# Moving the first quarter of W_in ahead of the keys of pair 1 in POOL's load order

## The chip, the cores and the metric

The kernel runs on one core of one Trainium2 chip. The metric is the device time of one execution in microseconds (us), as the median of several runs. A profiled execution also has a span: the time from its first to its last instruction on the core.

## What is computed

A gated recurrence over 768 steps in 4 batches and 8 heads of 48 channels makes y; y is the input x of a two-layer network with a gelu (tanh form) between the layers.

```python
for t in range(S):                       # S = 768
    state = alpha[:, :, t, :, None] * state + einsum('bhd,bhe->bhde', k[:, :, t], v[:, :, t])
    y[:, :, t] = einsum('bhd,bhde->bhe', q[:, :, t], state)
x = y.transpose(0, 2, 1, 3).reshape(B * S, H * D)      # 3072 x 384
h = x @ w_in                                           # w_in: 384 x 2048
g = 0.5 * h * (1 + tanh(c * (h + 0.044715 * h**3)))
out = g @ w_out                                        # w_out: 2048 x 384
```

All inputs and the output are float32. The kernel computes in bf16 and f16 with float32 sums.

## The kernel before

**Tiling.** The 768 steps are cut into 6 chunks of 128, and the 4 batches into two pairs of batches. A "pair" in the names of this kernel is one chunk of two batches, so there are 12: pair 0 and pair 1 are the first chunk of batches 0, 1 and 2, 3. For each pair the recurrence is done in chunked form:

- ACT takes the logarithm of alpha (`ln`), PE sums it along the chunk (`cum`), and ACT makes the exponentials `b`, `binv` and `bend`.
- DVE multiplies q by `b` and k by `binv` (`qp`, `kp`, line 354). For pairs 0 and 1 this is one instruction for each half of a pair, so two `qp` and two `kp`.
- PE transposes `qp` and `kp` (`qkT_ps`, line 364), and DVE or ACT copies the result from PSUM to SBUF (`qkT`, line 382).
- PE multiplies them (`at`, line 424), DVE masks (`atm`, line 431), PE makes y (`yps`, lines 470 and 473), ACT or DVE copies it to `x` (480), PE transposes it (`xT_ps`, 487) and DVE copies that to `xT` (491).
- For the state, the k of pairs 0 and 1 is turned back (`k_ps` on PE, 390; `kn`, 397) and multiplied with v (`kv`, 441).

**The network.** Layer 1 of a pair is 16 groups of three matmuls into `hT` (line 497), each followed by a gelu on ACT (`gT`, 503). Group `nt` uses columns of W_in from part `nt // 4`: W_in is loaded in four parts ("in 0" to "in 3"), and W_out likewise ("out 0" to "out 3"). Layer 2 (`acc`, 516) sums over the 16 groups.

**Who sets the order.** A planner, `Scheduler.order()`, runs when the program is built. Each task has a cost for the engines it can run on, a priority, and tasks and buffers that it waits for. Walking through estimated times, the planner fixes the order of all instructions on each engine. PE also gets filler matmuls (`idle`, line 222) where the plan has a gap early on. On the chip each engine then follows its own fixed list and waits on semaphores.

**Loads.** The pieces in `RINGS` are issued by the SP and ACT queues, in the order of that list: alpha, q and k of pair 0, then alpha and q of pair 1. All other loads are issued by POOL in the order of the tuple `LOADS`. Its names are read so:

- `gatea0` and `gatek0` are small copies on POOL that read a loaded tile (line 255), so that POOL issues nothing further before alpha, respectively k, of pair 0 has landed.
- `v0` is v of pair 0 (line 235). `pk1` is k of pair 1, in four pieces (`load_packed`, line 247). `in 0` is the first part of W_in (`load_w`, line 262).
- Numbers are the further pairs; `2a` and `2b` are halves of pair 2.

The planner numbers the loads in this order and gives each a time at which it lands:

```python
    if t.land is not None:
        wire = max(wire, t.end + W["dma"] - t.land) + t.land
        t.done = wire + t.late
```

**Buffers.** `BUFS` holds two PSUM buffers of tag `yk`: transposes of q and k, of x, the y and the kv all share these two, so a transposition waits until the last but one has been copied out. The tag `ff` (layer 1, layer 2, the filler) has four.

Of the kernel before, what the change touches and what calls it, by code (L numbers as in the profile page):

```python
# [136 lines left out]
class _Kernel:  # L137
# [3 lines left out]

    SPLIT = (2,)
    EARLY = (0, 1)
    LOADS = ('gatea0', 'v0', 'gatek0', 'pk1', 'in 0', 'in 1', 'in 2', 'v1', 'in 3', 'out 0', 'out 1', '2a', 'out 2', '2b', 'out 3', '3', '4', '5', '6', '7', '8', '9', '10', '11')

    PACKED, CUM_FF, R = (0, 1), (1,), 4
    RINGS = (('a', 0, 0, 'SP'), ('a', 0, 2, 'ACT'), ('a', 0, 1, 'SP'), ('a', 0, 3, 'ACT'), ('q', 0, 0, 'SP'), ('q', 0, 2, 'ACT'), ('q', 0, 1, 'SP'), ('q', 0, 3, 'ACT'), ('k', 0, 0, 'SP'), ('k', 0, 2, 'SP'), ('k', 0, 1, 'SP'), ('k', 0, 3, 'SP'), ('a', 1, 0, 'SP'), ('a', 1, 1, 'SP'), ('a', 1, 2, 'SP'), ('a', 1, 3, 'SP'), ('q', 1, 0, 'SP'), ('q', 1, 1, 'SP'), ('q', 1, 2, 'SP'), ('q', 1, 3, 'SP'))
# [389 lines left out]
    def tasks(self):  # L537
# [28 lines left out]
        for r, m, j, e in self.RINGS:  # L566
            loads[r, m, j] = s.add("load", {e: W["piece_issue"]}, n, self.load_packed(r, *pairs[m], j), land=W["piece"] + (0 if n else W["begin"]))
            n += 1
            if (r, m, j) == self.TABLE:
                s.add("table", {"ACT": W["table"]}, n, lambda e: self.act_set(LN_EXP))  # L570
        for step in self.LOADS:
            if step[0] == "v":
# [257 lines left out]
```

## Time and profile before

| what | value |
|---|---|
| median of 6 runs | 185.33 us (184.52 to 186.07) |
| the profiled execution, its time | 185.15 us |
| the profiled execution, its span | 183.4 us |
| PE (TensorE matmuls) busy | 175.7 us, 96% of the span |
| ACT (ScalarE) busy | 136.1 us, 74% |
| DVE (VectorE) busy | 104.8 us, 57% |
| POOL (GpSimd) busy, mostly issuing loads | 61.1 us, 33% |
| chain that ended last | PE 86%, DMA 8% |
| TensorE clock granted | 1.0 throughout |

"Busy" is time in instructions; PE overlaps instructions, so its share is not the share of its peak. The chain follows the execution back from its last instruction, at each step to what released it. The profile can also be asked for stretches of time, which is needed here: everything that the change touches lies in the first 30 us.

### The profile page before, as it was taken

What the parts mean: (1) busy time and instruction counts of PE and PEld (TensorE: products, weight loads), DVE (VectorE), ACT (ScalarE), POOL (GpSimd) and SP (SyncE); (2) the same over time, 40 slices, a digit from 0 to 9 for tenths busy, and PEclk for the clock granted to TensorE, in tenths of its full rate; (3) what the DMA queues carried; (4) which work ended last, traced back from release to release, by engine and by line L of the source; (5) the groups of instructions that cost most, each with busy time, mean ns of one, the idle gap of its engine ahead of it and who ended that gap; (6) DMA issues with size and microseconds to landing.
All of it is one profiled execution on the core that took longest, in us unless ns stands there. A gap on an engine that the chain in (4) does not pass through costs nothing.

```text
span 183.4 us, 4630 instructions
## 1 busy us (share of the span) xinstructions
PE 175.7 (96%) x1862; PEld 129.1 (70%) x1862; DVE 104.8 (57%) x232; ACT 136.1 (74%) x310; POOL 61.1 (33%) x68
## 2 busy tenths in 40 slices
PE   7886999999999999999999999999999999999993
PEld 2464868666686787688688769678677677686873
DVE  7776864065869896597499798298644715000000
ACT  3665979855888789859799768899789884491941
POOL 2599445985655556556660200000000000000000
DMA  5999999999999999999999985753271290311102
GB/s 141 202 235 176 187 227 205 205 220 170 188 275 187 165 226 195 179 226 202 180 211 231 186 205 119 104 114 68 51 168 49 43 202 4 88 43 46 43 0 86
DMA packets 51205, 27.76 MB, mean 151 GB/s; under 512 B 38832, under 2 KB 48240, under 8 KB 51184
## 3 DMA queue, kind: packets, MB, share of 16 engines
q0 software_dynamic: 32096, 17.70, 69.9%
q1 hardware_dynamic: 18512, 9.38, 21.6%
q10 hardware_dynamic: 576, 0.39, 0.7%
q8 instruction: 14, 0.23, 0.6%
q14 instruction: 7, 0.06, 0.1%
HBM read 25.17 MB, written 4.72 MB: 163 GB/s over the span
## 4 chain that ended last, share of the span: by engine, by line
PE 86%; DMA 8%; ACT 1%; POOL 1%; SPq 1%; DVE 0%; issue 0%; DVEq 0%; POOLq 0%
PE acc L516 34%; PE hT L497 33%; DMA k<-in_k_dram 5%; PE at L424 4%; PE qkT_ps L364 4%; PE yps L473 2%; PE yps L470 2%; PE kv L441 2%; PE cum L320 2%; DMA qkT<-kp 2%; DMA a<-in_alpha_dram 1%; PE xT_ps L487 1%; POOL k L247 1%; ACT L503 1%; PE cum L322 1%; SPq L247 1%
## 5 line engine op out<-in xcount | busy, mean ns | idle before, releaser
L497 PE MATMUL hT<-xT,w_in 128*128 128x256 bf16 x576 | 70.6, 273 | 0.4 <-ACT gT L503 0.4
L503 ACT ACTIVATE gT<-hT 128x256 bf16<-128x256 f32 x192 | 63.7, 386 | 8.8 <-PE hT L497 8.2
L516 PE MATMUL acc<-w_out,gT 128*128 128x384 bf16 (+1 forms) x400 | 68.8, 319 | 0.0
L497 PEld LDWEIGHTS <-w_in 128*128 128x128 bf16 x576 | 53.9, 98 | 8.2 <-issue 0.6
L516 PEld LDWEIGHTS <-gT 128*128 128x128 bf16 x400 | 36.8, 98 | 19.6
L431 DVE TENSOR_TENSOR atm<-at,ut 128x512 bf16<-128x512 f32 x48 | 31.0, 686 | 15.6 <-PE at L424 15.1
L354 DVE TENSOR_TENSOR qp<-q,b 128x768 bf16<-128x768 f32 (+1 forms) x15 | 11.8, 795 | 17.7 <-ACT b L343 13.8
L528 ACT COPY ot<-acc 128x384 f32<-128x384 f32 (+1 forms) x18 | 8.3, 462 | 13.9 <-PE acc L516 12.7
L235 POOL DMA_DIRECT2D v<-in_v_dram x13 | 14.6, 1123 | 9.6 <-PE hT L497 2.7
L235 POOL DMA_DIRECT2D k<-in_k_dram x11 | 12.2, 1108 | 11.3 <-DVE kp L354 4.6
L343 ACT ACTIVATE b<-cum 128x768 bf16<-128x768 f32 (+1 forms) x15 | 10.2, 684 | 6.6 <-PE cum L322 2.6
L235 POOL DMA_DIRECT2D q<-in_q_dram x11 | 12.2, 1112 | 7.3 <-DMA k<-in_k_dram 2.0
L235 POOL DMA_DIRECT2D a<-in_alpha_dram x11 | 12.2, 1112 | 6.4 <-DMA k<-in_k_dram 1.9
L213 ACT ACT_TABLE_LOAD x9 | 11.5, 1283 | 2.8 <-issue 2.6
L354 DVE TENSOR_TENSOR kp<-k,binv 128x768 bf16<-128x768 f32 (+1 forms) x15 | 11.7, 793 | 1.2 <-DMA k<-in_k_dram 0.9
L458 DVE TENSOR_TENSOR st<-stmp,bend 64x192 bf16<-64x192 f32 x32 | 11.3, 353 | 1.5
L456 DVE TENSOR_TENSOR stmp<-kv,st 64x192 f32<-64x192 f32 x32 | 11.3, 352 | 1.0 <-PE kv L441 0.7
L503 ACT ACT_TABLE_LOAD x9 | 11.5, 1283 | 0.2
L480 ACT CAST x<-yps 128x384 bf16<-128x384 f32 x15 | 7.2, 481 | 5.2 <-PE yps L473 5.1
L222 PE MATMUL idle<-zero 128*128 128x512 bf16 x28 | 9.6, 449 | 1.2 <-DVE blk L778 1.2
L382 DVE COPY qkT<-qkT_ps 128x1024 bf16<-128x1024 bf16 (+1 forms) x14 | 9.2, 687 | 2.4 <-PE qkT_ps L364 2.4
L343 ACT ACTIVATE binv<-cum 128x768 bf16<-128x768 f32 (+1 forms) x15 | 10.1, 683 | 0.0
(62 smaller groups left out, 160.2 us busy)
## 6 DMA issues: line engine op xcount, KB each, us to landing
out_dram<-ot SPq DMA_DIRECT2D x23, 192.0 KB, 3.5
a<-in_alpha_dram POOLq DMA_DIRECT2D x9, 384.0 KB, 13.1
q<-in_q_dram POOLq DMA_DIRECT2D x9, 384.0 KB, 13.4
k<-in_k_dram POOLq DMA_DIRECT2D x9, 384.0 KB, 13.3
v<-in_v_dram POOLq DMA_DIRECT2D x11, 192.0 KB, 13.4
w_in<-in_moe_w_in_dram POOLq DMA_DIRECT2D x4, 384.0 KB, 8.6
w_out<-in_moe_w_out_dram POOLq DMA_DIRECT2D x4, 384.0 KB, 11.3
a<-in_alpha_dram SPq DMA_DIRECT2D x6, 96.0 KB, 3.3
```

The lines of the kernel that those rows point to most:

```text
L213: nc.scalar.add_instruction(mybir.InstLoadActFuncSet(name=nc.get_next_instruction_name(), act_func_set_id=i, engine=mybir.EngineType.Activ ...
L222: self.nc.tensor.matmul(ps, self.zero[:, 0:self.C], self.zero, start=True, stop=True)
L235: (nc.sync if e == "SP" else nc.gpsimd).dma_start(u[n][:, lo:hi].rearrange("t b h d -> t (b h) d"), src)
L343: self.nc.scalar.activation(u[n].rearrange("t i h d -> t i (h d)")[:, lo:hi], cum, AF.Exp, scale=1.0 if n == "b" else -1.0)
L354: self.nc.vector.tensor_tensor(out, rows, b, op=ALU.mult)
L382: self.copy(e)(t, ps)
L431: self.nc.vector.tensor_tensor(u["atm", i][:, o], u["at", i][o], self.ut[:, None, :].to_broadcast([self.C, self.H // 2, self.C]), op=ALU.mult)
L456: nc.vector.tensor_tensor(s[ps], acc, old[ps, :, fs], op=ALU.add)
L458: nc.vector.tensor_tensor(new[ps, :, fs], acc, u["bend"][ps, i, :, None].to_broadcast([64, H // 2, D]), op=ALU.mult)
L497: self.nc.tensor.matmul(h, self.w_in[:, j, nt * self.C:(nt + 1) * self.C], self.xT[c][:, j, lo:hi].rearrange("p g t -> p (g t)"), start=j ...
L503: return lambda e: self.nc.scalar.activation(self.gT[c % self.NG][:, nt, lo * self.C:hi * self.C], f.pop(("h", c, lo, nt)), AF.Gelu_apprx_ ...
L516: self.nc.tensor.matmul(f["acc", c, b][:, lo:hi], self.gT[c % self.NG][:, nt, b * self.C:(b + 1) * self.C], self.w_out[:, nt, lo:hi], star ...
```

## The change

One name moves in the tuple `LOADS`: `'in 0'` goes ahead of `'pk1'`, so POOL issues the first part of W_in directly behind `gatek0`, ahead of the four pieces of k of pair 1.

```diff
     SPLIT = (2,)
     EARLY = (0, 1)
-    LOADS = ('gatea0', 'v0', 'gatek0', 'pk1', 'in 0', 'in 1', 'in 2', 'v1', 'in 3', 'out 0', 'out 1', '2a', ...
+    LOADS = ('gatea0', 'v0', 'gatek0', 'in 0', 'pk1', 'in 1', 'in 2', 'v1', 'in 3', 'out 0', 'out 1', '2a', ...
```

The description that came with the change says that the order of all engines stays. The built programs differ in more than POOL's loads, because the planner now has another landing time for k. Those are all the differences:

| engine | before | after |
|---|---|---|
| POOL | k of pair 1 x4, W_in 0, 1, 2 | W_in 0, k of pair 1 x4, W_in 1, 2 |
| DVE | qp, kp, xT, kp, xT, qp (qp and kp of pair 1, xT of pair 0) | qp, qp, xT, kp, xT, kp |
| PE | transposes of qp, 2 fillers, transposes of kp, layer 1, transposes of qp, layer 1, transposes of kp | transposes of qp, 2 fillers, transposes of qp, layer 1, transposes of kp, layer 1, transposes of kp |

"Layer 1" stands for one group of three matmuls each time. ACT and SP keep their lists.

More of the change, by code (lines that the diff above doesn't have):

```diff
@@ L143 @@
     EARLY = (0, 1)
-    LOADS = ('gatea0', 'v0', 'gatek0', 'pk1', 'in 0', 'in 1', 'in 2', 'v1', 'in 3', 'out 0', 'out 1', '2a', 'out 2', '2b', 'out 3', '3', '4', '5', '6', '7', '8', '9', '10', '11')
+    LOADS = ('gatea0', 'v0', 'gatek0', 'in 0', 'pk1', 'in 1', 'in 2', 'v1', 'in 3', 'out 0', 'out 1', '2a', 'out 2', '2b', 'out 3', '3', '4', '5', '6', '7', '8', '9', '10', '11')
     PACKED, CUM_FF, R = (0, 1), (1,), 4
```

## The prediction

> **What bounds the kernel now.** The page comes first: TensorE (PE) is busy for 175.7 of 183.4 us, and the chain that ended last is 86% PE and 8% DMA. The DMA share is where loads can still set the end, so I follow the chain in order of time from the start. Its columns are start in us, length in us, what.
>
> ```profile
> 8.56 1.62 POOL k L247 x3
> 10.19 5.77 DMA k<-in_k_dram
> 15.95 0.03 issue
> ...
> 16.08 0.56 DVE kp L354
> 16.64 0.28 DVE xT L491
> 16.91 0.04 issue
> 16.95 0.38 PE qkT_ps L364 x4
> 17.34 0.43 PE idle L222 x2
> ...
> 19.84 0.33 PE hT L497 x3
> 20.16 0.33 PE at L424 x8
> ...
> 24.66 0.01 issue
> 24.68 0.50 PE hT L497 x3
> ```
>
> The last of the four pieces of k of pair 1, issued by POOL, lands at 10.19 + 5.77 = 15.96. From 16.95 on the chain stays on PE, without a gap over 0.04 us up to 28.7, where layer 1 of pair 1 runs. So a shift of PE at 20.16 (the first `at` of pair 1) has no idle time to sink into. It also meets no later load: the DMA pieces left in the whole chain are the first alpha, these two of k (5%) and the transposes qkT<-kp near the end, which move with PE.
>
> The timeline of VectorE (DVE) shows what k holds up (start, length, what, the wait ahead of it in brackets):
>
> ```profile
> 14.57 0.56 DVE L354 TENSOR_TENSOR qp<-q,b 128x384 bf16<-128x384 f32 x1 [0.97 <-ACT x L480]
> 16.08 0.56 DVE L354 TENSOR_TENSOR kp<-k,binv 128x384 bf16<-128x384 f32 x1 [0.94 <-DMA k<-in_k_dram]
> 16.55 0.35 DVE L491 COPY xT<-xT_ps 128x384 bf16<-128x384 bf16 x1
> 16.82 0.55 DVE L354 TENSOR_TENSOR kp<-k,binv 128x384 bf16<-128x384 f32 x1
> 17.28 0.35 DVE L491 COPY xT<-xT_ps 128x384 bf16<-128x384 bf16 x1
> 17.55 0.55 DVE L354 TENSOR_TENSOR qp<-q,b 128x384 bf16<-128x384 f32 x1
> 18.11 1.89 DVE L382 COPY qkT<-qkT_ps 128x512 bf16<-128x512 bf16 x3
> ```
>
> Both xT copies stand behind a kp, though their inputs were transposed by 15.7. They gate the first layer-1 product of pair 0 at 18.07. Hence **k of pair 1 gates layer 1 of both pairs**.
>
> The timeline of POOL gives the issues:
>
> ```profile
> 8.54 2.20 POOL L247 DMA_DIRECT2D k<-in_k_dram  x4
> 10.73 2.25 POOL L262 DMA_DIRECT2D w_in<-in_moe_w_in_dram  x3
> ```
>
> With the times to landing of the DMA view, the first part of W_in lands at 10.73 + 6.5 = 17.2, the second at 19.5, the third at 21.4 (starts 11.47 and 12.23; POOL waits for them at 19.81 and 21.68). So part 0 lands 0.9 us before its first use. Earlier arrival buys nothing unless xT comes earlier too.
>
> **What the skill says.** "DMA: Bandwidth & Descriptors", section "Queues, rings and completion order": each DMA engine takes its queues in turn, and within a queue descriptors are consumed in ring order. The trace agrees in the order of landings on POOL's queue: k, then W_in 0, 1, 2. Its section "Anatomy of one DMA — SWDGE (gpsimd) path" prices a POOL load at 2.0 us plus bytes / 436e3; an estimate for 96 KB of k is 2.2 us. The trace shows 5.1 to 6.0, so these loads stand in a line and the fit is only a floor. "PSUM — Partial Sum Buffer", section "Engine vs sequencer instructions", calls the vector engine's queue strictly first in, first out; the xT at 16.55 behind the waiting kp agrees.
>
> **The change part by part.**
>
> 1. POOL: one issue of W_in (756 ns) goes ahead of four issues of k (551 to 572 ns). W_in 0 is issued at 8.54, k at 9.29 to 11.5 instead of 8.54 to 10.73. Sum unchanged, so W_in 1 starts as before at 11.47. Nothing on SP's queue or ACT's is moved, but the four q pieces that SP issues from 7.42 to 9.27 (landed by about 14.4, 5.1 to 5.6 us each) now share the DMA engines with W_in 0 rather than k. POOL reuses a completion semaphore every eighth load, so W_in 3 (14.17) will wait for W_in 0 instead of the first k piece (13.7). W_in 0 should land near 15, so W_in 3 is issued some 0.8 us later. Its data stand behind W_in 1, 2 and v until 22.8, which covers that; without the cover the product at 24.68 would be 0.8 late.
>
> 2. When does k land now, called K? It is behind 384 KB of W_in. Low bound: only the issue counts, 15.96 + 0.75 = 16.7. Even lower, if the line is shorter once q has drained: last issue 10.94 plus the shortest time of a piece, 5.1, gives 16.0. If bytes are conserved, the pair of loads ends when it ended before, K = 17.2. High bound: a full spacing of two W_in loads (17.2 to 19.5 is 2.3) is put ahead of k, K = 18.3. W_in 0 had landed only 1.3 behind k where its successors need 1.9 to 2.3, so part of it had already moved while k finished; that head start is lost to k. I take **K = 17.5**, between 17.2 and 15.96 + 1.9 = 17.9.
>
> 3. The planned order does move, on DVE and PE, against the plain reading of "stays": the second qp and one xT go ahead of both kp (qp, qp, xT, kp, xT, kp), and both groups of qp transposes ahead of those of kp. From K on, with the pitches of the DVE timeline: kp at K + 0.13, second xT K + 0.60 to 0.95, kp K + 0.87 to 1.42. PE: qp transposes at K + 0.99 (the buffer is freed by that xT), product K + 1.29, kp transposes K + 1.62, product K + 1.84, last kp transposes K + 2.17. DVE copies: 0.60 apart from K + 1.42, the last ends at K + 3.3. PE after 2.17: 0.29, product 0.33, k_ps 0.27, product 0.33, then `at` at **K + 3.4**. Before it was 20.16 = K + 4.2. So 0.8 us goes from behind k to ahead of it: the first qp transposes (0.39) and the fill (0.43) are done during the wait. They were paid before too.
>
> 4. Sum: `at` moves by 17.5 + 3.4 − 20.16 = **+0.74 us**, and the end with it. ACT's table load, 17.98 before, can start near 16.9 and stays hidden; the first gelus wait for PE. The profiled execution took 185.15 with a span of 183.4, 0.18 below the median of 185.33. I expect a span of 184.1, a time of 185.9 for such an execution and a median of **186.1**.
>
> The formula has one unknown: shift = K − 16.76. The 0.5% that a measurement of this kernel can tell from no change is 0.93 us: slower needs K over 17.7, faster K under 15.8.
>
> **The rivals.**
>
> A, the forecast: a shared line, K between 17.2 and 17.9, 185.8 to 186.5. For it: landings in order and 1.9 to 2.3 apart. Chance 0.50, of which 0.13 lies above 17.7.
>
> B, a full load ahead: q slows W_in 0 and k then pays a whole spacing, K near 18.3, shift +1.54, 186.9. It ends on the slow side, and decides from K = 17.7. For it: q's pieces and W_in 0 overlap from 10 to 14, a window that moved 221 to 246 GB/s, and k no longer gets its share there. Against: the same bytes were done by 17.2. Chance 0.28.
>
> C, latency rather than bytes: K = 16.7, shift −0.06, 185.3; the issue's 0.75 is just paid by the work moved ahead. Against: times to landing growing from 5.1 to 10.5 along the line. Chance 0.14.
>
> D, the wait shrinks: with q out of the way k's pieces land quickly and K falls below 15.8, shift −1 or more, 184.3. Around 5 us SP's k pieces took 3.1 us to land; but then W_in 0 would have to be through by 13, within a microsecond of v's landing (5.0 + 7.2 = 12.2). Chance 0.08, of which 0.03 remains within 0.5%.
>
> That the early part changes nothing it was loaded for is in all four: its first product stays behind k, through xT.
>
> **How the numbers follow.** Slower: 0.13 of A and 0.28 of B, plus 0.03 for noise along the rest of PE's chain, 0.44. Faster: 0.05 of D and 0.02 of noise, 0.07. Within: 0.49. The range goes from C less 0.2 of spread (the six runs lie within 0.8 of the median) to B, rounded: 185.1 to 187.0.
>
> **What would show it.** In the profile after: k's landing in the chain near 17.5 (15.96 before); DVE with two qp and an xT ahead of the waiting kp; its wait for k about 1.6 us from 15.9 (0.94 before); the first layer-1 product near K + 1.3, 18.8 instead of 18.07; `at` near 20.9; the pair-1 products and everything after later by that. A landing near 16.7 makes C right, over 17.7 B. It would be wrong in kind if `at` moved and the end did not (slack I didn't see after 28.7), or if the end moved with `at` at its place.

## The result and the profile after

| | before | after |
|---|---|---|
| median of all runs | 184.97 us (70 runs) | 185.81 us (33 runs) |
| ratio after / before, 95% interval | | 1.0032 [1.0017, 1.0047] |
| profiled execution, its time | 185.15 us | 186.63 us |
| profiled execution, its span | 183.4 us | 184.9 us |

The change makes the kernel 0.3% slower. That is clear of noise, and below the 0.5% within which the forecast placed it. The profiled execution is one of the longer ones, 0.8 us above the median. In 8 of 34 runs (the profiled one counted) the mean granted TensorE clock was 0.991 or less, and those took 187.4 to 190.7 us; the ratio leaves them out, and experiments 2, 5, 6 and 10 deal with their cause.

The chain of waits of the changed kernel, in order of time (start us, length us, what):

```profile
8.27 0.74 POOL w_in L262
9.01 1.67 POOL k L247 x3
10.68 7.72 DMA k<-in_k_dram
...
18.52 0.56 DVE kp L354
...
19.40 0.38 PE qkT_ps L364 x4
19.78 0.33 PE hT L497 x3
...
21.87 0.33 PE at L424 x8
...
26.16 0.21 PE idle L222
26.37 0.33 PE hT L497 x3
```

The last piece of k is issued 0.5 us later than before and lands 2.4 us later, at 10.68 + 7.72 = 18.40: it travelled for 7.7 us instead of 5.8. From there to `at` it is 21.87 − 18.40 = 3.47 us, where it was 4.20.

The timeline of DVE (start, length, what, the wait ahead of it) shows both parts of the change, the later k and the new order:

```profile
15.66 1.03 DVE L354 TENSOR_TENSOR qp<-q,b 128x384 bf16<-128x384 f32 x2 [1.48 <-DMA q<-in_q_dram]
16.60 0.35 DVE L491 COPY xT<-xT_ps 128x384 bf16<-128x384 bf16 x1
18.52 0.56 DVE L354 TENSOR_TENSOR kp<-k,binv 128x384 bf16<-128x384 f32 x1 [1.57 <-DMA k<-in_k_dram]
19.00 0.35 DVE L491 COPY xT<-xT_ps 128x384 bf16<-128x384 bf16 x1
19.26 0.55 DVE L354 TENSOR_TENSOR kp<-k,binv 128x384 bf16<-128x384 f32 x1
19.82 1.89 DVE L382 COPY qkT<-qkT_ps 128x512 bf16<-128x512 bf16 x3
```

Two qp and an xT are done before k. The second xT still stands behind a kp, so layer 1 of pair 0 begins only at 19.78. The wait for k is 1.57 us (0.94 before). In the first line q, issued by SP, is what the first qp waits for, until 15.66; before, the first qp began at 14.57. That this comes from the change is not shown: q's last piece landed from 14.4 to 15.9 in the seven profiles with one whole part of W_in ahead of k, and from 13.7 to 16.1 in the five with none.

And the timeline of POOL:

```profile
8.27 0.74 POOL L262 DMA_DIRECT2D w_in<-in_moe_w_in_dram  x1 [0.28 <-issue]
9.00 2.23 POOL L247 DMA_DIRECT2D k<-in_k_dram  x4
...
16.96 0.74 POOL L262 DMA_DIRECT2D w_in<-in_moe_w_in_dram  x1 [2.66 <-DMA w_in<-in_moe_w_in_dram]
```

The last part of W_in is issued at 16.96 (14.17 before), because it now waits for the first part to land, near 16.7. It still lands at 24.84, 0.2 later than before, since its data stand in line anyway.

### The profile page after: what moved, and what is told of

Read it like the earlier page. It is cut to its first block, busy times and chain, and to the rows that moved or that the text cites. A ratio compares the mean times of both kernels' runs of the same rounds, so it can differ in the third digit from the quotient of the medians.

```text
span 184.9 us, 4631 instructions
## 1 busy us (share of the span) xinstructions
PE 176.3 (95%) x1862; PEld 129.6 (70%) x1862; DVE 104.8 (57%) x232; ACT 136.1 (74%) x310; POOL 60.7 (33%) x68
## 4 chain that ended last, share of the span: by engine, by line
PE 85%; DMA 9%; POOL 1%; ACT 1%; SPq 1%; issue 1%; DVE 0%; DVEq 0%; POOLq 0%
PE acc L516 34%; PE hT L497 32%; DMA k<-in_k_dram 6%; PE at L424 4%; PE qkT_ps L364 3%; PE yps L473 2%; PE yps L470 2%; PE kv L441 2%; PE cum L320 2%; DMA qkT<-kp 2%; DMA a<-in_alpha_dram 1%; PE xT_ps L487 1%; POOL k L247 1%; ACT L503 1%; PE cum L322 1%; SPq L247 1%
## 5 line engine op out<-in xcount | busy, mean ns | idle before, releaser
L354 DVE TENSOR_TENSOR qp<-q,b 128x768 bf16<-128x768 f32 (+1 forms) x15 | 11.8, 795 | 19.0 <-ACT b L343 17.5
```

The costliest lines, as they stand in the source:

```text
L354: self.nc.vector.tensor_tensor(out, rows, b, op=ALU.mult)
```

## The experiments

Of each edit the lines that matter are shown, with remarks behind `#` that the code doesn't have. Nearly all readings come down to three times of each profile: **K**, when k of pair 1 lands; the start of the first `at` of pair 1; and the start of the 13th layer-1 group of pair 0, the first that uses the last part of W_in (called W3). The last two are starts in the timeline of PE, which gives `at` 0.06 us earlier than the chain. Experiments 7, 8 and 10 have their times in their own sections.

| kernel | K | at | at − K | W3 lands | 13th group | span − 13th group |
|---|---|---|---|---|---|---|
| before | 15.96 | 20.10 | 4.14 | 24.63 | 24.68 | 158.7 |
| before, 12 | 15.80 | 19.94 | 4.14 | 24.58 | 24.62 | 158.8 |
| after | 18.40 | 21.80 | 3.40 | 24.84 | 26.21 | 158.7 |
| after, 1 | 17.98 | 21.39 | 3.41 | 24.53 | 25.79 | 158.7 |
| after, 11 | 17.84 | 21.25 | 3.41 | 24.50 | 25.65 | 158.8 |
| 2, loads only | 17.23 | 21.38 | 4.15 | 23.86 | 25.78 | 158.6 |
| 3, order only | 15.23 | 18.87 | 3.64 | 24.16 | 24.20 | 158.8 |
| 4, a third ahead | 16.58 | 19.98 | 3.40 | 24.34 | 24.39 | 159.2 |
| 5, after with fillers | 17.01 | 20.41 | 3.40 | 23.72 | 24.82 | 158.7 |
| 6, loads only with fillers | 17.26 | 21.40 | 4.14 | 23.68 | 25.80 | 158.6 |
| 9, issue only | 15.37 | 19.21 | 3.84 | 24.62 | 24.67 | 158.8 |

What the table says: with the order of before `at` starts at K + 4.14, with the new one at K + 3.40, whatever K is. (In 3 and 9 k came so early that DVE was still busy with qp and xT, so `at` hung on those.) The 13th group starts at `at` + 4.40, **or** 0.05 after W3 lands if that is later. The end comes some 158.7 us after that group, in all but one.

### 1 and 11: the changed kernel again

> The changed kernel once more. K is when k of pair 1 lands; it was 15.96 us in the profile of before and 18.40 in that of the changed kernel, whose execution (186.63 us) was 0.8 us over its median. Theory (K sets PE, and K varies from run to run with the queue of loads): at starts at K + 3.4 to 3.5 whatever K is; with K between 17 and 18.4 the span is about 183.4 + (K - 16.8) less 0.2, so 183.4 to 184.9; ratio to before near 1.003. Rival (K is 18.4 each time, and most of the delay is won back further down): K = 18.4 again, with a span below 184.

> The changed kernel once more, for another K. Theory: at at K + 3.47, the 13th layer-1 group 4.5 us later, and the end 158.5 us after that group's start, with K between 17.0 and 18.4. Rival: another step sets at, K + 3.47 is missed by over 0.2 us.

Measured: ratio 1.0047 [1.0029, 1.0065] for the first; K 17.98 and 17.84, `at` at K + 3.41 in both, spans 184.5 and 184.4. The theory holds, and the rival (a K of 18.4 and a win further down) falls. The profiled run of the first took 186.31 against its median of 185.58, that of the second 186.13, so all three profiles show an execution that is longer than the usual one. They took 168.2 to 168.3 us more than their K. By that, the 185.68 us of the changed kernel's median without the runs at a low clock belong to a K near 17.4, which is an estimate.

### 12: the kernel before again

> The kernel before once more, for another K. Theory: at at K + 4.20 with K between 15.2 and 16.5, and the 13th layer-1 group at the later of at + 4.5 and the landing of the last part of W_in; the end 158.7 us after that group's start. Rival: K varies as much as 1 us above that, so that the difference of the two kernels is one of chance.

Measured: K 15.80, `at` 4.14 later, span 183.4. The 13th group began at 24.62, with W3 landed at 24.58, where `at` + 4.40 gives 24.34. The chain of this execution goes through W3 and not through the wait for k:

```profile
14.35 10.23 DMA w_in<-in_moe_w_in_dram
24.58 0.05 issue
24.62 0.50 PE hT L497 x3
```

So in the kernel before **W3 ends the start-up**, and PE's own chain is just about as late (24.34 here, 24.50 in the first profile).

### 2: only the loads

```diff
         order = self.s.order()          # planned with the LOADS of before
+        first, k = self.loads["w", "in", 0], self.loads["k", 1, 0]
+        order.remove(first)
+        order.insert(order.index(k), first)
```

> Only POOL's order is changed (first part of W_in ahead of k of pair 1); DVE and PE keep their order of before. Theory (the reorder hides 0.8 us behind the wait for k): at starts at K + 4.2, so with K near 17.5 at 21.7, 1.5 us later than before, ratio 1.007 to 1.008. Rival (the reorder on DVE and PE is worth nothing): ratio as for the changed kernel, 1.003.

Measured: 1.0157 [1.0111, 1.0202], far more than expected. The profile, however, has `at` at K + 4.15 as expected, and its execution took 186.26 us, 0.8% over before. The other five runs took 188.3 to 189.8 us with a mean granted clock of 0.982 to 0.991, and the 1.0157 takes in two of these. The timeline of PE, in the profile with a clock of 0.999, has a gap of 2.25 us where the kernel before has one of 1.28 (first line before, second line this run):

```profile
16.95 0.38 PE L364 MATMUL qkT_ps<-ident,qp 128*128 128x128 bf16 x4 [1.28 <-DVE xT L491]
18.23 0.38 PE L364 MATMUL qkT_ps<-ident,qp 128*128 128x128 bf16 x4 [2.25 <-DVE xT L491]
```

This called for experiments 5 and 6.

### 3: only the order of the engines

The planner works with the changed `LOADS`, and then W_in's first part is put back behind k in POOL's list.

> Only the order on DVE and PE is changed (both qp and one xT ahead of both kp); POOL loads k ahead of W_in as before. K should be 16.0 again and at should start at K + 3.4 = 19.4, 0.8 us earlier than before. Theory: that gain does not reach the end, since the last part of W_in lands at 24.6 and its first product at 24.68 waits for it (it waited 0.2 already): ratio 0.999 to 1.001, with a wait of about 0.8 us ahead of the 13th layer-1 group. Rival (PE's chain passes every shift on): the end moves by the full -0.8 us, ratio 0.9957.

Measured: 1.0003 [0.9992, 1.0013]. PE in the timeline, around the 13th group:

```profile
23.09 0.38 PE L222 MATMUL idle<-zero 128*128 128x512 bf16 x1
24.20 0.50 PE L497 MATMUL hT<-xT,w_in 128*128 128x256 bf16 x3 [0.73 <-DMA w_in<-in_moe_w_in_dram]
```

PE is there early and waits 0.73 us for W3. The gain of the new order is real, and by itself it is worth nothing at the end: the theory holds, and the rival (−0.8 us) falls.

### 4: a third of the bytes ahead of k

```diff
+        rest = Task("load", {}, 0, w0(1, 3))      # k-tiles 1 and 2 of part 0, issued behind k
+        rest.engine, rest.load, first.emit = "POOL", None, w0(0, 1)     # first: k-tile 0, ahead of k
+        order.insert(order.index(k[3]) + 1, rest)
```

> As the changed kernel, but only one of the three k-tiles of the first part of W_in (128 KB of 384 KB) goes ahead of k of pair 1, the other two behind it; one POOL issue more. Theory (bytes in one line): K is delayed by a third, near 16.0 + 0.5 = 16.5 plus up to 0.3 for the extra issue; at at K + 3.4, about 20.0 to 20.3; ratio 0.999 to 1.001. Rival (what delays k is being second in line, latency and not bytes): K as in the changed kernel, 17.5 or more, ratio 1.003.

Measured: K 16.58, `at` 19.98, ratio 1.0014 [1.0001, 1.0026], a little over the expected range. K lies between the profiles with none ahead (15.2 to 16.4) and those with a whole part ahead (17.0 to 18.4), as the theory of one line of bytes has it. It is one execution, so it doesn't show that the cost is in proportion; and more bytes are also more packets, which no experiment told apart.

### 9: only the later issue of k

```diff
+        busy = Task("busy", {}, 0, lambda e: [nc.gpsimd.memset(self.scratch, 0.0) for _ in range(3)])
+        order.insert(order.index(k[0]), busy)     # ahead of k; W_in 0 stays behind k
```

> DVE and PE in the order of the changed kernel; POOL loads k of pair 1 ahead of W_in as before, but first spends some 0.6 to 0.75 us on three memsets of an unused tile, so that k is issued late and nothing is put ahead of it in the line. Theory (bytes ahead of k cost, not the later issue; v of pair 0 keeps the line busy to 12.2): K within 0.4 us of the 15.2 to 16.0 of the runs without W_in ahead; ratio 1.000 to 1.002. Rival (the later issue is what delays k): K about 0.75 us or more later than with the plain order, 16.5 and over, like the run with a third of W_in 0 ahead.

Measured: K 15.37, within the 15.2 to 16.4 of the other profiles with no W_in ahead, though k was issued from 8.98 on, as in the changed kernel. The later issue alone shows no delay of k, and the 16.5 and over of the rival did not come. The ratio is 1.0021 [1.0005, 1.0037], just over what was expected; in the profile PE waited 0.89 us for W3.

### 10: two parts ahead of k

> As the changed kernel, with the second part of W_in also ahead of k of pair 1. Theory (each 384 KB of W_in ahead of k costs it about 1.6 to 2.0 us; six runs with one part ahead had K from 17.0 to 18.4, mean 17.5, three with none 15.2 to 16.5): K from 19.0 to 20.0, at at K + 3.5, the 13th layer-1 group about 4.5 us after at. Rival (k pays mostly once for not being first): K under 18.5.

Measured: one execution of 190.06 us, with a mean clock of 0.982 and K 19.15, so the theory holds for k. But `at` came at 24.50, K + 5.35 instead of 3.40. The row of the granted clock in this profile says why (40 slices of 4.7 us, tenths of full speed, 9 is full):

```profile
PEclk9999579999999999999999999999999999999999
```

So does the table of stages (stage, its length, busy time of PE, of PE's weight loads, DVE, ACT and POOL with instructions, granted clock, DMA share, GB/s):

```profile
16.00:18.00 2.00, 0.81 (x6) 0.42 (x6) 0.00 (x0) 1.52 (x2) 0.54 (x2) 1.00 1.10 206
18.00:20.00 2.00, 0.00 (x0) 0.00 (x0) 0.73 (x2) 0.35 (x1) 2.00 (x4) 0.83 2.00 172
20.00:22.00 2.00, 1.85 (x13) 1.54 (x13) 1.41 (x4) 0.38 (x1) 2.00 (x3) 0.50 1.50 196
...
24.00:26.00 2.00, 2.00 (x21) 1.33 (x20) 0.69 (x1) 1.15 (x3) 0.90 (x1) 0.50 1.31 224
26.00:28.00 2.00, 2.00 (x22) 1.78 (x21) 1.70 (x5) 1.89 (x7) 0.89 (x1) 0.96 1.20 244
```

And its timeline of PE:

```profile
16.26 0.59 PE L222 MATMUL idle<-zero 128*128 128x512 bf16 x2
20.15 0.58 PE L364 MATMUL qkT_ps<-ident,qp 128*128 128x128 bf16 x4 [3.29 <-DVE xT L491]
20.53 0.84 PE L497 MATMUL hT<-xT,w_in 128*128 128x256 bf16 x3
```

PE's fillers ended at 16.85, and then it waited 3.29 us for k. The clock fell to one half within that wait. The mean of 0.83 from 18 to 20 us stands for 0.68 us at one half (2 × 0.17 × 2), so it fell near 19.3, when PE had been idle for about 2.5 us; the 0.96 from 26 to 28 us puts its return near 26.2. In between a layer-1 group takes 0.84 us instead of 0.49. The Trainium skill describes this in "TensorE: Matmul & The Clock Gate", section "What's actually happening": the array's clock is halved after an idle window of about 3.4 us, the window runs freely, and it takes a busy window to get the full clock back. The halved stretch in this trace, 6.8 us, agrees with two such windows: the first still held the end of the wait, up to 20.15, and PE was busy throughout the second. On the fall the trace differs from the page: in the 3.4 us before it PE was not idle for a whole window, it still worked for about 0.8 us (the first line of the table).

### 5 and 6: the gap on PE filled

In 5 the planner's two filler matmuls between the two groups of qp transposes become eight. In 6 eight are put ahead of the first qp transposes in the kernel of experiment 2.

```diff
+        next(t for t in order[at:] if t.kind == "fill").emit = self.fill(8)     # 5; at: the first qp transposes
+        order.insert(order.index(self.tq1), more)                               # 6; more emits self.fill(8)
```

> As the changed kernel, with 8 filler matmuls instead of 2 between the two groups of qp transposes, so that TensorE works through most of its wait for k (1.6 us in the profile). Theory (the gap in TensorE's work makes the granted clock fall in a part of the runs; 8 of 34 runs of the changed kernel had a mean clock of 0.991 or less and took 187.4 to 190.7 us): no run under a mean clock of 0.998, all runs between 184.5 and 186.7, ratio 1.003 to 1.005 as before without those runs. Rival (the low clocks have nothing to do with the gap): they come as often, 1 run in 4.

> As the kernel with only POOL's loads reordered (ratio 1.0157, with 5 of 6 runs at a clock of 0.982 to 0.991), with 8 filler matmuls ahead of the first qp transposes, in the gap of 2.25 us that TensorE had there. Theory: the clock stays at 1.0, and what is left is the shift through k alone: at at K + 4.2, ratio 1.007 to 1.008 (0.8 us above the changed kernel's). Rival (the extra time has another cause than the clock): ratio stays near 1.015.

Measured: no run of either has a clock under 0.998. In 6 that is 8 runs, against 5 of 6 with a low clock in 2, and the ratio falls from 1.0157 to 1.0063 [1.0038, 1.0087]. With the fillers the gap of the loads-only kernel is down to this:

```profile
18.26 0.38 PE L364 MATMUL qkT_ps<-ident,qp 128*128 128x128 bf16 x4 [0.95 <-DVE xT L491]
```

Together with the trace of 10, where the clock falls inside the gap, this shows that the gap on PE lowers the clock, though 6 was run on another chip than 2. For the changed kernel it is likely and not shown: 8 of its 41 runs without fillers, the six of experiment 1 and that of 11 counted, had a low clock, and with that share 10 runs have none by chance about one time in nine.

The changed kernel with fillers has 1.0059 [1.0033, 1.0086] and one run of 187.32 at full clock, above the expected range. In its profile the eight fillers end at 18.1, which suits a K of 17.0; behind a later q they end later and may cost time. With 10 runs its interval doesn't tell it from the 1.0047 of experiment 1.

One expectation stays open. Loads only with fillers should be 0.8 us, 0.4%, above the changed kernel. The profiles show that difference from K on (4.14 against 3.40), but the ratios, 1.0063 against 1.0032 to 1.0059, show 0.04 to 0.3% with intervals as wide. In both profiles of that kernel k landed early (17.2 and 17.3), and whether that was chance or has a cause wasn't settled.

### 7: work for the early part of W_in

```diff
+        for t in self.kp1:                       # DVE: both kp behind the second xT
+            order.remove(t)
+            order.insert(order.index(x1) + 1 + self.kp1.index(t), t)
+        for t in l1[1:4]:                        # PE: four layer-1 groups ahead of the kp transposes
+            order.remove(t)
+            order.insert(order.index(self.tk1[0]), t)
```

> As the changed kernel, but DVE takes both xT ahead of both kp, and PE takes the first four layer-1 groups (all that use the first part of W_in) ahead of the kp transposes, so the early part of W_in has work before k lands. Theory (only work ahead of k is won; 1.0 us of layer 1 and the last qp transposes, 0.4 us, move there): at at about K + 2.6, so with K of 17.5 to 18 the 13th layer-1 group is near 25.0, and the end 0.3 to 0.5 us after that of before; ratio 1.000 to 1.002. No run under a clock of 0.998, since the gap is shorter. Rival (the first four groups wait for the landing of W_in 0, near 16.5, or for gelu, and give nothing): ratio 1.004 as the changed kernel.

Measured: 1.0027 [1.0015, 1.0040], over the expected range, with K 17.28 in the profile, `at` at K + 2.8, the 13th group at 24.69. One of 22 runs had a low clock, against the expectation of none. DVE shows where 0.2 us of the expected gain went:

```profile
17.39 1.03 DVE L354 TENSOR_TENSOR kp<-k,binv 128x384 bf16<-128x384 f32 x2 [0.80 <-DMA k<-in_k_dram]
18.34 1.94 DVE L382 COPY qkT<-qkT_ps 128x512 bf16<-128x512 bf16 x3
```

The copy of the second qp transposes, ready by 17.4, stands behind both kp, so three copies remain after them. In this profile layer 1 started at 17.26, just as k landed, but the median does not come down to that of before: W_in's early part, now used early, doesn't make good what it costs k.

### 8: half of v behind W_in

DVE and PE in the new order, POOL as before, but v of pair 1 in two loads, the second behind W3.

> DVE and PE as in the changed kernel, POOL as before, but v of pair 1 is loaded in two halves, the second behind the last part of W_in. In the run with only the engine order changed, PE came to the 13th layer-1 group at 23.4 and waited 0.73 us for the last part of W_in (24.16). Theory (W_in's last landing now ends the start-up): with 96 KB less ahead of it that part lands about 0.7 us earlier, near 23.5, and the end moves by -0.4 to -0.7 us; ratio 0.996 to 0.998. Rival (something else ends last, or the half v is then late for y of the second batch, which needs it near 25.0): ratio 1.000.

Measured: 1.0010 [0.9995, 1.0025], no gain. Its profile is of an execution in which the loads came late: k landed at 16.44, DVE's first qp of pair 1 began at 16.19 (14.38 in experiment 3), and the 13th group at 25.09, some 0.6 us after W3 (24.46). So there q and k, not W3, ended the start-up. W3 itself came at 24.46 and not near the expected 23.5; in this execution W_in's first part, too, landed late (18.03, against 16.7 in experiment 3). Whether this holds for the usual execution is open. No variant tried beats the kernel before.

## Why the prediction was right, step by step

**The sum.** A median shift of +0.74 us was forecast. Measured are +0.84 in the medians of all runs, +0.7 with the runs at a low clock left out (185.68), and +0.6 by the ratio (0.0032 × 185). "Within 0.5%" came true, but the forecast gave it 0.49 against 0.44 for slower, so the call itself was little better than even. What the runs support is the sum behind it.

**K (step 2), the term with all the uncertainty.** The seven profiles with one whole part of W_in ahead of k, counting 2, 5, 6 and 7, have K from 17.01 to 18.40, mean 17.57; 17.5 was taken. With none ahead five profiles have 15.23 to 16.44, mean 15.76; with a third 16.58; with two 19.15. So 384 KB of W_in cost k about 1.8 us, and the next 384 KB 1.6, the latter from one execution. The bound of 17.2 (the pair of loads ends when it ended before) is passed by six of the seven, by three of them by less than 0.1; the bound of 18.3 was passed once, by 0.1.

A landing is the last of a load's 16 completions, and in some executions one of the 16 lags. In the three profiles of the changed kernel the last completion for k's last piece came 1.1 to 1.5 us after the fifteenth, in the other four of the seven at most 0.5 us after it. In experiment 8, with k in front, the lag is 1.15 us, so it doesn't need W_in ahead. Counted to the fifteenth completion K has a mean of 16.85 with one part ahead and 15.20 with none, so the price of the 384 KB, 1.65 us, does not rest on the lag. But of the 2.4 us between the first two profiles, about 0.8 is a difference in the lag (1.20 against 0.44).

**C, that only the later issue counts**, is ruled out by 9 (K 15.37). D didn't occur. B fits single executions: by the sign that the prediction named, "over 17.7 B", all three profiles of the changed kernel (18.40, 17.98, 17.84) speak for B. For the median the estimate of 17.4 speaks for A.

**The chain from K to `at` (step 3)** was K + 3.4 and measured 3.47 in the chain three times of three. That 0.7 to 0.8 us move ahead of k through the planner's new order, against the words "the order stays", is shown by the two values of `at` − K.

**"No idle time to sink into" failed, by 0.17 us.** The 13th group in the chain of before is 0.50 long and in that of after 0.33. The difference was a wait for W3, which I read as work. The timeline of the kernel before has it on PE's weight load:

```profile
24.67 0.22 PEld L497 LDWEIGHTS <-w_in 128*128 128x128 bf16 x3 [0.40 <-DMA w_in<-in_moe_w_in_dram]
```

The filler ahead was still running until 24.66, so the chain shows no idle time; but without the wait the group would have overlapped it, as it does after. It is the greater part of why `at` moved by 1.71 us and the end by 1.5. Step 1 had named this product and this load, and only its landing, 14.17 + 10.46 = 24.63, was not set against the 24.68. For a gain it would have mattered far more: in 3 `at` came 1.2 us earlier (0.7 of it from an earlier k) and the end did not. A rival built on a gain through the order had no room, and the prediction did not see that.

**POOL's step 1** was right in kind and short in size: W3's issue was put 0.8 us late and was 2.8 late, since W_in's first part landed near 16.7 and not 15. The cover named for it held.

**q** was said to share the engines with W_in 0. Its last piece landed near 14.4 before and 15.5 after, a difference within the spread of either order (see above), so the sharing is not shown. The later q cost nothing here, since the work it feeds is done during the wait for k.

**The clock** was missing from the prediction. A longer wait on PE need not only shift what follows: in experiment 10 it halved the clock for 6.8 us, and the low mean clocks of a part of the other runs fit the same cause.

## What to carry to other kernels

A load that nobody waits for yet is not free to move ahead: put in front of the load that gates the start-up, it delays that one, here by 1.6 to 1.8 us for 384 KB, and the early bytes are idle if their user waits for the same gate. Before counting a gain from an earlier engine, look for the transfer that lands just as that engine arrives; two limits within 0.3 us of each other look like one in the chain. Where a change lengthens a wait on TensorE, look at the granted clock of every run, not only at the profile.

## What the runs showed of the hardware beyond what was expected

- In experiment 10 the clock fell when TensorE had been idle for about 2.5 us. Low mean clocks in other runs mostly went with longer gaps in the profile: 5 of 6 runs with a gap of 2.25 us (2), 8 of 41 with two gaps of 0.87 and 1.58 us (after), 1 of 22 with one of 1.07 us (7), 1 of 115 with one of 1.28 us (the runs of before beside the experiments). How long the gap was in the runs with a low clock isn't known, since K varies and only 10 was profiled in one. And 2 of the 20 runs of 9, whose profile has no such gap, had a mean clock of 0.991 and took 185.6 and 185.7 us; their cause is open. A mean of 0.991 over 186 us is about 3.3 us at half speed, worked out as 0.009 × 186 × 2.
- The time of landing of one load differs by 1.4 us between executions of the same order of loads (17.01 to 18.40). Much of that is one completion of 16: in the profile after, 15 of the 16 for the last piece of k had come by 17.20, and the last came at 18.40; in experiment 5 they came at 16.95 and 17.01. In the executions with this lag W_in's first part, too, had one late completion (15.55 and 16.68 after). Which of the DMA engines it is, and why, the profile doesn't tell.
